# Seven block products for the output projection of the last two batches: fused attention and gated MLP on one core

## The chip, the core and the metric

The kernel runs on one core of a Trainium2 chip: TensorE (PE) multiplies matrices into PSUM, VectorE (DVE), ScalarE (ACT) and GpSimd (POOL) work element by element, and the queue of SyncE (SP) issues nearly all DMAs. The metric is device time in microseconds (us) of one execution, as the median of several runs; lower is better.

## The reference

```python
scores = scale * np.matmul(q, k.transpose(0, 1, 3, 2))      # 4 batches, 12 heads, 448 tokens, 64 wide
scores = np.where(mask, -1000000000.0, scores)              # causal
attn = np.exp(scores - np.max(scores, axis=-1, keepdims=True))
attn = attn / (np.sum(attn, axis=-1, keepdims=True) + 1e-09)
x = np.matmul(attn, v)      # -> (B * S, H * D): 1792 tokens x 768
g = x @ w_gate              # 768 x 1536
silu = g * (1.0 / (1.0 + np.exp(-g)))
return silu * (x @ w_val) @ w_out     # w_out: 1536 x 768
```

All inputs and the output are float32.

## The kernel before, in words

**Tiling.** A batch is one chunk of T = 448 tokens. Activations lie transposed, features on 128 partitions and tokens along the row, so a matmul is 128x128 weights by 128x448 activations. Every float32 operand is split into a high part (a rounded copy) and a low part (operand minus high part), and each product takes three matmuls: high by high, high by low, low by high (`mm3`, L1150 to L1152). The copy runs on ACT, DVE or POOL (`copies`, L400, L403, L406), the subtraction on DVE or POOL (`binary`, L422, L425). A weight tile is 128x768 (`wraw` the raw tile, `whl` its two parts, four buffers each), kept in DRAM as `wr`.

**Stages.** Attention of batch b runs beside the MLP of batch b-1. For batches 0 and 1, `moe` does gate, up and output projection. The last two batches, A = 2 and B_ = 3, share their gate and up products: `early` (L1274) computes the block for A alone, spills partial sums to DRAM (`ks`), and `pair` (L1390) does the rest in five further block products for each of n = 0 to 5, over sums of weights (S1 to S4, `S1hl` and so on their split parts) and sums of activations that `operands` (L1323) prepares (`T2hl`, slabs of the tile `last`). The results are the hidden activations: hA (batch 2; twelve tiles f) and hB (batch 3; in `xs` and `hraw` buffers).

**Output projection of batches 2 and 3.** It is a matrix product in 2x2 by 2x2 blocks: upper and lower half of the 768 output rows (3 tiles m each), first and second half of the 1536 hidden features (6 tiles f each), batch A and B_. Eight block products of 3 x 6 x 3 = 54 matmuls do it. Two of them, first half of the features of A for all six m, run in `early` as soon as these features exist (PSUM tiles MO2_0 to MO2_5, then ACT copies them to `part` and SP spills them as `ko`). The other six run in `outputs` (L1574): for every m, A's second half (with `back`, the spilled part, added by DVE at L1606) and both halves of B_.

**What sets the order.** Every engine works through its instructions in program order. That order is written by `Planner.run`, a list scheduler that plays the kernel through with a cost table: at each step it takes, on the engine that can start earliest, the first ready operation by due time. A due time is written by hand (the stage lengths LEN, the leads WLEAD and BOOST) plus an offset for each group (the table SHIFT, some 300 numbers). Operations that may run on several engines go to the one that would end earliest. Buffers come in rings (CAPS: `whl` 4, `wraw` 4, `wide` 3, `tmp` 2, `t` 2, `osb` 2); an operation that needs a buffer waits for the last user of the oldest.

**Turned heads.** For batches in VIA the softmax weights are transposed through DRAM (`turn`, L862): DVE writes the tile `w`, SP sends it out, SP reads it back. For an odd head the returned data goes into a second buffer, `x`.

## Time and profile before

| what | value |
|---|---|
| runs | 634.48, 634.03, 632.47 us, median 634.03 |
| profiled execution | 632.45 us, of which the span from first to last instruction is 630.7 us |
| granted TensorE clock | 1.00 in all stages (the upper of its two levels, 2.4 GHz) |
| PE busy | 623.1 us, 99% of the span |
| DVE, ACT, POOL busy | 517.0 (82%), 416.9 (66%), 251.3 (40%) |
| DMA | 136.07 MB, mean 216 GB/s |

In the profile PE is the matmuls and PEld the weight loads of TensorE. Matmul durations overlap, since matmuls are pipelined; the distance from one start to the next tells their pace. An engine's waits are listed by what ended them.

### The profile page before, as it was taken

What the parts mean: (1) busy time and instruction counts of PE and PEld (TensorE: products, weight loads), DVE (VectorE), ACT (ScalarE), POOL (GpSimd) and SP (SyncE); (2) the same over time, 40 slices, a digit from 0 to 9 for tenths busy, and PEclk for the clock granted to TensorE, in tenths of its full rate; (3) what the DMA queues carried; (4) which work ended last, traced back from release to release, by engine and by line L of the source; (5) the groups of instructions that cost most, each with busy time, mean ns of one, the idle gap of its engine ahead of it and who ended that gap; (6) DMA issues with size and microseconds to landing.
All of it is one profiled execution on the core that took longest, in us unless ns stands there. A gap on an engine that the chain in (4) does not pass through costs nothing.

```text
span 630.7 us, 11116 instructions
## 1 busy us (share of the span) xinstructions
PE 623.1 (99%) x3590; PEld 561.2 (89%) x3590; DVE 517.0 (82%) x1168; ACT 416.9 (66%) x1001; POOL 251.3 (40%) x301
## 2 busy tenths in 40 slices
PE   8999999999999999999999999999999999999997
PEld 5557999999999999999999998889999999999997
DVE  5998999989998998988998889799988889975210
ACT  6998658958997678577687899775554454561110
POOL 3665543444356455435445453440034324440000
PEclk9999999999999999999999999999999999999999
DMA  8979597888996987576677877886444343236301
GB/s 284 333 245 335 139 384 276 281 318 293 307 362 167 320 267 246 149 249 220 177 224 252 271 239 201 251 283 230 136 121 130 129 131 102 86 109 190 105 18 70
DMA packets 72666, 136.07 MB, mean 216 GB/s; under 512 B 18080, under 2 KB 45472, under 8 KB 72608
## 3 DMA queue, kind: packets, MB, share of 16 engines
q1 hardware_dynamic: 72304, 135.04, 65.5%
q8 instruction: 28, 0.46, 0.3%
q10 hardware_dynamic: 304, 0.33, 0.2%
q14 instruction: 30, 0.25, 0.1%
HBM read 98.34 MB, written 37.00 MB: 215 GB/s over the span
## 4 chain that ended last, share of the span: by engine, by line
PE 83%; DVE 6%; DMA 5%; ACT 4%; issue 1%; POOL 0%; ACTq 0%; SPq 0%; DVEq 0%; POOLq 0%
PE M L1150 10%; PE M L1151 10%; PE M L1152 10%; PE MO L1150 9%; PE MO L1151 9%; PE MO L1152 9%; PE S L618 7%; PE O L1017 5%; DMA wr<-wr 3%; PE T L842 2%; PE O L1062 2%; PE Bb L1467 2%; PE Bb L1466 2%; PE Bb L1468 2%; PE Be L1468 1%
## 5 line engine op out<-in xcount | busy, mean ns | idle before, releaser
L1150 PE MATMUL M<-xh,whl 128*128 128x448 f32 x360 | 133.7, 371 | 0.9 <-ACT s L1289 0.7
L1152 PE MATMUL M<-xh,whl 128*128 128x448 f32 x360 | 130.4, 362 | 0.0
L1151 PE MATMUL M<-xl,whl 128*128 128x448 f32 x360 | 130.4, 362 | 0.0
L422 DVE TENSOR_TENSOR whl<-wraw,whl 128x768 fp32r<-128x768 f32 x86 | 83.9, 983 | 21.1 <-ACT whl L400 20.7
L681 ACT ACTIVATE p<-p,m 128x192 f32<-128x192 f32 (+3 forms) x180 | 91.1, 509 | 2.3 <-DVE m L669 2.0
L400 ACT ACTIVATE whl<-wraw 128x768 fp32r<-128x768 f32 x72 | 60.2, 840 | 34.1 <-PE MO L1152 19.8
L1150 PEld LDWEIGHTS M<-xh,whl 128*128 128x128 f32 x360 | 67.5, 188 | 7.8 <-ACT s L1289 2.8
L1152 PEld LDWEIGHTS M<-xh,whl 128*128 128x128 f32 x360 | 67.5, 187 | 4.7
L669 DVE CUSTOM_DVE_ANT_0 p<-S,masks 128x192 f32<-128x192 f32 (+3 forms) x180 | 68.3, 424 | 3.5 <-PE S L618 3.3
L1151 PEld LDWEIGHTS M<-xl,whl 128*128 128x128 f32 x360 | 67.6, 188 | 3.8
L1150 PE MATMUL MO<-h,whl 128*128 128x448 f32 x162 | 59.7, 369 | 0.0
L1151 PE MATMUL MO<-h,whl 128*128 128x448 f32 x162 | 58.7, 362 | 0.0
L1152 PE MATMUL MO<-h,whl 128*128 128x448 f32 x162 | 58.5, 361 | 0.0
L735 ACT ACTIVATE p<-p,rec 128x192 f32<-128x192 f32 (+3 forms) x128 | 53.9, 478 | 4.6 <-DVE rec L692 4.5
L1136 DVE SCALAR_TENSOR_TENSOR wraw<-wide,top 128x768 uint32<-128x768 uint32 x36 | 36.0, 1000 | 1.9 <-ACT top L400 1.8
L900 DVE STREAM_TRANSPOSE w<-p 128x256 f32<-128x256 f32 (+2 forms) x120 | 36.3, 354 | 0.6 <-ACT p L735 0.3
L618 PEld LDWEIGHTS S<-KS,QS 64*128 64x128 f32 (+1 forms) x432 | 29.6, 174 | 6.3 <-issue 4.1
L681 ACT ACTIVATION_READ_ACCUMULATOR p<-p,m 128x1 f32 (+1 forms) x180 | 34.1, 190 | 0.0
L425 POOL TENSOR_TENSOR whl<-wraw,whl 128x768 fp32r<-128x768 f32 x16 | 29.5, 1848 | 9.2 <-DVE whl L422 3.1
L1150 PE MATMUL MO<-last,whl 128*128 128x448 f32 x90 | 33.1, 368 | 0.0
L1151 PE MATMUL MO<-last,whl 128*128 128x448 f32 x90 | 32.6, 363 | 0.0
L1152 PE MATMUL MO<-last,whl 128*128 128x448 f32 x90 | 32.6, 362 | 0.0
(386 smaller groups left out, 1527.5 us busy)
## 6 DMA issues: line engine op xcount, KB each, us to landing
wide<-in_w_dram SPq DMA_DIRECT2D x36, 768.0 KB, 6.8
wraw<-wr SPq DMA_DIRECT2D x66, 384.0 KB, 4.1
wr<-wraw SPq DMA_DIRECT2D x36, 384.0 KB, 4.2
wr<-wr SPq DMA_DIRECT2D x24, 384.0 KB, 3.8
x<-dO SPq DMA_DIRECT2D x12, 608.0 KB, 6.0
vraw<-in_v_dram SPq DMA_DIRECT2D x24, 256.0 KB, 4.4
qraw<-in_q_dram SPq DMA_DIRECT2D x23, 224.0 KB, 5.0
kraw<-in_k_dram SPq DMA_DIRECT2D x23, 224.0 KB, 5.0
```

Of the source, the lines that this page charges most:

```text
L400: nc.scalar.activation(out(), in_(), AF.Copy, scale=scale)
L422: r["DVE"] = (cost("DVE", "two", n), lambda: nc.vector.tensor_tensor(out(), a(), b(), alu))
L618: nc.tensor.matmul(st[u + y][f"S{i}"][:r], Q[:, q0 : q0 + r], K[:, :q1_] if y else K[:, S - q1_ :], start=z == 0, stop=z == len(passes) - 1)
L669: nc.vector.tensor_tensor_reduce(p[:r], s[f"S{i}"][:r], mask[:r, maskX - q0 : maskX - q0 + q1_] if h % 2 else back[:r, P - min(q1_, P) : P ...
L681: nc.scalar.activation(p[:r], p[:r], AF.Exp, bias=peak(i)[:r], scale=-1.0, accum_out=sums[u % NR][:r, i : i + 1],)
L735: nc.scalar.activation(p[:r], p[:r], AF.Copy, scale=rec[u % NR][:r, i : i + 1])
L900: nc.vector.transpose(to, src)
L1017: nc.tensor.matmul(o, s["VS"][:, j, :m], p, start=x == 0, stop=x == len(todo) - 1)
L1136: nc.vector.scalar_tensor_tensor(w["raw"].bitcast(U32), z, 13, top, ALU.logical_shift_right, ALU.bitwise_or)
L1150: nc.tensor.matmul(out[:, :n], a[:, w], xhi, start=first, stop=False, skip_group_check=True)
L1151: nc.tensor.matmul(out[:, :n], a[:, w], xlo, start=False, stop=False, skip_group_check=True)
L1152: nc.tensor.matmul(out[:, :n], l[:, w], xhi, start=False, stop=bool(last), skip_group_check=True)
```

## The change

The output projection of the two batches takes seven block products. `early` keeps one (upper rows, first half, batch A: MO2_0 to MO2_2 in place of MO2_0 to MO2_5), and `outputs` does six, phase0 to phase5, each over sums or differences of weight blocks (`So`, `top`, added in place from phase to phase) and of activation blocks (`xs`, `T1hl`, `hraw` tiles). The sums are VectorE or GpSimd instructions like the splits (`binary`; `minus` is a new form of the subtraction, on VectorE alone). Three PSUM results run through several phases: ScalarE copies a state out (`ou2`, `ou3`) before the next product adds to it. To have batch 2's hidden features for the sums, `early` and `pair` spill them (`kh`), and SP reads six of the twelve back into `xs`. Some signs change (`activate` takes a sign). The constant ACC is empty, so the DMA branch `gather` isn't used.

An odd head's turned weights return to the buffer that they left from. The planner runs three times: after a pass, `latest` works out for each operation the latest start that delays nothing in that pass, and this is the due time of the next; SHIFT, with new numbers throughout, is added in the last pass alone. `place_all` fixes the order of the buffers in memory. The diff, cut:

```diff
-LEN = [57.293, 137.864, 266.214, 76.452, 83.944, 91.479]
+LEN = [57.293, 137.864, 266.214, 76.452, 83.944, 75.0]
...
+PASSES = 2
 SPARE = [2]
-PLACES = {(1, 1): 7}
+PLACES = {(1, 1): 0}
...
-    "": 0.77, "attention0": -24.87, "attention1": -21.61, "attention10": 3.28, "attention11": 4.59, "attention12": 0.29, "attention13": -0.26,
...
+    "": 0.17, "attention0": -6.39, "attention1": -3.11, "attention10": -1.47, "attention11": -7.66, "attention12": -0.15, "attention13": 0.08,
...
+    def latest(self, order):
+
+        end, after = max(o.end for o in order), None
+        for o in sorted(order, key=lambda o: o.start)[::-1]:
+            t = end
+            for d in o.outs:
+                lag = 0.0 if o in d.soft else o.extra + (LAT[o.eng] if d.eng != o.eng else (0.0 if o.eng == "PE" else 0.13))
+                t = min(t, d.late - lag)
+            for r in o.uses:
+                if r.next is not None:
+                    t = min(t, r.next.owner.late - o.extra - LAT[o.eng])
+            if o.eng == "PE":
+                if after is not None:
+                    t = min(t, after.late)
+                after = o
+            o.late = t - (o.end - o.start)
+
     def run(self, caps):
+        nd, extra = [o.nd for o in self.ops], [o.extra for o in self.ops]
+        order = self.once(caps)
+        for i in range(PASSES):
+            self.latest(order)
+            for o, n, x in zip(self.ops, nd, extra):
+                o.nd, o.extra, o.due = n, x, o.late + (o.shift if i == PASSES - 1 else 0.0)
+                for r in o.uses:
+                    r.left, r.end, r.next = len(r.users), 0.0, None
+            order = self.once(caps)
+        return order
...
-        spare = lambda a, n: [Res(f"lent{a}")] if at is not None else [Res("wide")]
-        rS = spare(4, 3) if odd else spare(0, 4)
+        rS = [Res(f"lent{2 * at + odd}")] if at is not None else [Res("wide")]
...
-        rd = op({"SP": (0.35, back), "kb": ND // 2}, due(6.6), [wr], rP if odd else [], [rD] + ([] if odd else rS))
+            s["turned"] = s["w"][:, :ND]
+            nc.sync.dma_start(s["turned"], s["d"])
+        rd = op({"SP": (0.35, back), "kb": ND // 2}, due(6.6), [wr], [], [rD] + rS)
...
+    def minus(n, out, a, b):
+
+        return {"DVE": (cost("DVE", "two", n), lambda: nc.vector.scalar_tensor_tensor(out(), a(), -1.0, b(), ALU.mult, ALU.subtract)), "port": True}
...
-    keepO = [dpool.tile([P, T], F32, tag=f"ko{m}", name=f"ko{m}") for m in range(KD)]
+    keepO = [dpool.tile([P, T], F32, tag=f"ko{m}", name=f"ko{m}") for m in range(HK)]
+    keepH = [dpool.tile([P, T], F32, tag=f"kh{f}", name=f"kh{f}") for f in range(NF)]
...
-        for m in range(KD):
+            kept["h", f] = spill(keepH[f], lambda f=f: ps[A, f, "t"], at(4 * f + 6), t3, rt)
+        for m in range(HK):
...
+                kept["h", f] = spill(keepH[f], lambda: ps["t21", n], at(9), t3, rt)
...
+        def first_sum(k):
+            res = [Res(f"xs{2 * k}"), Res(f"xs{2 * k + 1}")]
+            ld = op({"SP": (0.3, lambda: nc.sync.dma_start(xs[k], keepH[k])), "kb": 224}, at(HK) - AHEAD - 6, [kept["h", k]], res)
...
+                 op(binary(T, lambda: xs[k], lambda: xs[k], t_, ALU.add), at(HK) - AHEAD + 0.1 * k, [ld, o], [], res + r_))
...
+            a = op(copies("sbuf", T, to[0], lambda: xs[k], -1.0), at(HK) - AHEAD + 1 + 0.1 * k, [d], alloc[:1], res + (rs[:1] if not alloc else []))
+            l = op(minus(T, to[1], lambda: xs[k], lambda: raw(to[0]())), at(HK) - AHEAD + 2 + 0.1 * k, [a], alloc[1:],
+                   res + rs[:1] + (rs[1:] if not alloc else []))
...
+        def second_sum(k):
...
+                 op(binary(T, lambda: xs[k], lambda: xs[k], t_, ALU.add), at(2 * HK) - AHEAD + 0.1 * k, split + [o], [], res + r_))
+            to = (lambda: xh[k], lambda: xl[k])
+            ops_[2, k], places[2, k] = halves(lambda: xs[k], to, at(2 * HK) - AHEAD + 1 + 0.1 * k, [d], res, [Res(f"xh{k}"), Res(f"xl{k}")]), to
...
+        def third_sum(k):
...
+                 op(binary(T, t_, t_, t2, ALU.add), at(3 * HK) - AHEAD + 0.1 * k, [o, o2, sums_["x", k][0]], [], r_ + r2))
+            to = (lambda: hh("T3", k), lambda: hl("T3", k))
+            ops_[3, k], places[3, k] = halves(t_, to, at(3 * HK) - AHEAD + 1 + 0.1 * k, [d], r_, [Res(f"hh{k}"), Res(f"hl{k}")]), to
...
+        def plain(k):
...
+            ops_[4, k], places[4, k] = halves(t_, to, at(4 * HK) - AHEAD + 0.1 * k, [o], r_, rs), to
...
+        def fourth_sum(k):
...
+                d = op(binary(T, lambda: xs[k], lambda: raw(hh("A2", k)), lambda: xs[k], ALU.add), at(5 * HK) - AHEAD - 2 + 0.1 * k, split + [a], [], res + [ra])
+                d = op(binary(T, lambda: xs[k], lambda: xs[k], lambda: raw(hl("A2", k)), ALU.add), at(5 * HK) - AHEAD - 1 + 0.1 * k, [d, l], [], res + [rl])
...
+            ops_[5, k], places[5, k] = halves(lambda: xs[k], to, at(5 * HK) - AHEAD + 0.1 * k, [d], res, [Res(f"xh{k}"), Res(f"xl{k}")], -1.0), to
...
+        def divide(key, src, due, deps, res):
...
+            a = op(copies("sbuf", WC, new, src), due - 6 * WLEAD, deps, [rhl], res)
+            l = op(binary(WC, lambda: hls[key][:, 1], src, lambda: raw(hls[key][:, 0])), due - 5 * WLEAD, [a], [], res + [rhl])
+            return [a, l], rhl
...
+        def phase0(m):
+            src, ld, rw = fetch((0, m), W(m, 1), at(m) - 12 * WLEAD)
+            wo, rhl = divide((0, m), src, at(m), [ld], [rw])
+            rc = Res("MMS"[m])
+            last = product(0, m, ("c", m), "MMS"[m], rc, True, lambda k: (hA[k + HF], (lambda: hh("A2", k), lambda: hl("A2", k))), wo, rhl, [])
...
+            result(A, m, at(m + 1), [last, ld], [rc, rp], lambda: ps["c", m][:, :T], lambda: ps["back", m], scale=-0.5)
...
+        def phase1(m):
+            if "S" not in ACC:
+                s2, l2, r2 = fetch((1, m), W(m + HK, 0), at(HK + m) - 13 * WLEAD)
+                s3, l3, r3 = fetch((2, m), W(m + HK, 1), at(HK + m) - 13 * WLEAD)
...
+                d = op(binary(WC, new, s2, s3, ALU.add), at(HK + m) - 8 * WLEAD, [l2, l3], [rS], [r2, r3])
+            wo, rhl = divide((1, m), lambda: sums_[m], at(HK + m), [d], [rS])
+            re_ = Res("STO"[m])
+            last = product(1, m, ("e", m), "STO"[m], re_, True, lambda k: (ops_[1, k], places[1, k]), wo, rhl, [])
...
+        def phase2(m):
+            src, ld, rw = fetch((3, m), W(m, 0), at(2 * HK + m) - 12 * WLEAD)
+            wo, rS = sums_["s", m]
+            d = op(binary(WC, lambda: sums_[m], lambda: sums_[m], src), at(2 * HK + m) - 8 * WLEAD, [ld, *wo], [], [rS, rw])
...
+            last = product(2, m, ("b", m), "XXM"[m], rb, True, lambda k: (ops_[2, k], places[2, k]), wo, rhl, [])
+            ld, rp = back[m]
+            B = lambda: ps["b", m][:, :T]
+            g = op({"DVE": (two, lambda: nc.vector.scalar_tensor_tensor(B(), ps["back", m], 2.0, B(), ALU.mult, ALU.add))}, at(2 * HK + m + 1) - BOOST,
+                   [last, ld], [], [rb, rp])
+            ru = Res("vraw")
+            u = scaled(("ou2", m), "vraw", "vraw", ru, B, at(2 * HK + m + 1), [g], [rb])
+            upper[m] = (u, rb, ru)
...
+        def phase3(m):
+            s2, l2, r2 = fetch((4, m), W(m, 0), at(3 * HK + m) - 13 * WLEAD)
+            s3, l3, r3 = fetch((5, m), W(m + HK, 0), at(3 * HK + m) - 13 * WLEAD)
+            d = op(binary(WC, s3, s2, s3), at(3 * HK + m) - 8 * WLEAD, [l2, l3], [], [r2, r3])
...
+            last = product(3, m, ("b", m), None, rb, False, lambda k: (ops_[3, k], places[3, k]), wo, rhl, [u2])
+            ru3 = Res("tmp" if m else "t")
+            u3 = scaled(("ou3", m), "tmp" if m else "t", "tmp", ru3, B, at(3 * HK + m + 1), [last], [rb])
+            pe, re_ = lower[m]
+            e = result(B_, m + HK, at(3 * HK + m + 2), [pe, u3], [re_, ru3], lambda: ps["e", m][:, :T], lambda: ps["ou3", m])
...
+        def phase4(m):
+            src, ld, rw = fetch((6, m), W(m, 1), at(4 * HK + m) - 12 * WLEAD)
+            wo, rS = sums_["s", m]
+            d = op(binary(WC, lambda: sums_[m], src, lambda: sums_[m]), at(4 * HK + m) - 8 * WLEAD, [ld, *wo], [], [rS, rw])
...
+            last = product(4, m, ("e", m), None, re_, False, lambda k: (ops_[4, k], places[4, k]), wo, rhl, [e])
+            _, _, ru, u2 = upper[m]
+            result(B_, m, at(4 * HK + m + 1), [last, u2], [re_, ru], lambda: ps["e", m][:, :T], lambda: ps["ou2", m])
...
+        def phase5(m):
+            src, ld, rw = fetch((7, m), W(m + HK, 1), at(5 * HK + m) - 12 * WLEAD)
+            wo, rhl = divide((5, m), src, at(5 * HK + m), [ld], [rw])
+            u3, rb, _, _ = upper[m]
+            last = product(5, m, ("b", m), None, rb, False, lambda k: (ops_[5, k], places[5, k]), wo, rhl, [u3])
+            result(A, m + HK, at(5 * HK + m + 1), [last], [rb], lambda: ps["b", m][:, :T], final=m == HK - 1)
...
```

On PE, the end of the first half's projection in `early` is where the removed products stood. MO2_m is the PSUM tile of output tile m of batch 2, h its features, Be0_0 the first product of pair 0. Before:

```order
L1151 MATMUL MO2_3_6087<-h9_5929,whl102_5977 128x448
L1152 MATMUL MO2_3_6087<-h8_5911,whl102_5977 128x448
L1150 MATMUL MO2_3_6087<-h10_5983,whl102_5977 128x448
L1151 MATMUL MO2_3_6087<-h11_6001,whl102_5977 128x448
L1152 MATMUL MO2_3_6087<-h10_5983,whl102_5977 128x448
L1466 MATMUL Be0_0_6172<-last2_5282,S1hl0_6147 128x448
L1467 MATMUL Be0_0_6172<-last2_5282,S1hl0_6147 128x448
L1468 MATMUL Be0_0_6172<-last2_5282,S1hl0_6147 128x448
```

Now, at the same place:

```order
L1198 MATMUL MO2_2_6098<-h2_5620,whl100_6014 128x448
L1196 MATMUL MO2_1_6078<-h8_5953,whl98_5932 128x448
L1197 MATMUL MO2_1_6078<-h9_5971,whl98_5932 128x448
L1198 MATMUL MO2_1_6078<-h8_5953,whl98_5932 128x448
L1518 MATMUL Be0_0_6115<-last2_5386,S1hl0_6096 128x448
L1519 MATMUL Be0_0_6115<-last2_5386,S1hl0_6096 128x448
L1520 MATMUL Be0_0_6115<-last2_5386,S1hl0_6096 128x448
```

Pair 0 begins beside MO2_1 and MO2_2, where it began between MO2_3 and MO2_5; MO2_3 to MO2_5 are gone from this place.

On DVE, a stretch in the last stage. Before, it splits weight tiles (`whl`, the low part) and adds up outputs (`osb`):

```order
L1606 SCALAR_TENSOR_TENSOR osb2_1_7349<-MO2_1_7273,back1_7248 128x448
L422 TENSOR_TENSOR whl136_7344<-wraw136_7241,whl136_7344 128x768
L422 TENSOR_TENSOR whl139_7373<-wraw139_7292,whl139_7373 128x768
L403 TENSOR_SCALAR whl138_7414<-wraw138_7313 128x768
L1606 SCALAR_TENSOR_TENSOR osb2_2_7420<-MO2_2_7375,back2_7266 128x448
L422 TENSOR_TENSOR whl138_7414<-wraw138_7313,whl138_7414 128x768
```

Now, around the split of phase 2's first weight tile (hl2_0):

```order
L481 TENSOR_TENSOR hraw5_7177<-hraw5_7177,xs5_76 128x448
L481 TENSOR_TENSOR xs4_75<-xs4_75,hraw4_6958 128x448
L481 TENSOR_TENSOR hl2_0_7362<-So0_7156,hl2_0_7362 128x768
L1240 SCALAR_TENSOR_TENSOR T1hl1_7144<-xs4_75,T1hl0_7139 128x448
L481 TENSOR_TENSOR xs3_74<-xs3_74,h7_6834 128x448
L481 TENSOR_TENSOR xs4_75<-xs4_75,hraw4_6958 128x448
L481 TENSOR_TENSOR xs5_76<-xs5_76,hraw5_7177 128x448
L481 TENSOR_TENSOR h7_7388<-hraw3_6789,h6_7366 128x448
```

Between the splits of weights now stand sums of activations and the low parts of these sums, which the products of the same phases wait for.

## Rows read from the trace of the kernel before

**Rows 1.** The page's first part: busy us (share of the span) and instructions.

```profile
PE 623.1 (99%) x3590; PEld 561.2 (89%) x3590; DVE 517.0 (82%) x1168; ACT 416.9 (66%) x1001; POOL 251.3 (40%) x301
```

**Rows 2.** Windows: busy us and instructions by engine, clock, DMA share, GB/s.

```profile
core 0: us, PE busy (x) PEld busy (x) DVE busy (x) ACT busy (x) POOL busy (x), PEclk, DMA share, GB/s
0.00:45.00 45.00, 42.55 (x304) 25.75 (x306) 36.49 (x130) 38.95 (x126) 24.75 (x44) 1.00 0.88 301
45.00:376.00 331.00, 330.62 (x2019) 304.10 (x2016) 299.15 (x738) 256.82 (x652) 158.11 (x188) 1.00 0.79 258
376.00:480.00 104.00, 103.03 (x541) 94.33 (x540) 92.33 (x180) 68.23 (x140) 33.54 (x37) 1.00 0.66 203
480.00:507.00 27.00, 27.00 (x136) 25.03 (x134) 21.59 (x31) 12.45 (x21) 10.09 (x9) 1.00 0.33 113
507.00:536.00 29.00, 28.90 (x145) 27.03 (x145) 25.13 (x36) 13.15 (x22) 10.64 (x10) 1.00 0.39 126
536.00:560.00 24.00, 24.00 (x122) 22.50 (x121) 19.54 (x29) 13.49 (x23) 9.57 (x10) 1.00 0.32 102
560.00:585.00 25.00, 25.00 (x127) 23.43 (x126) 14.49 (x19) 8.66 (x14) 4.65 (x4) 1.00 0.51 159
585.00:630.70 45.70, 42.05 (x211) 39.06 (x209) 8.31 (x11) 5.14 (x8) 0.00 (x0) 1.00 0.17 59
```

**Rows 3.** Timeline of PE in pair 5: start us, us, instruction.

```profile
563.28 0.36 PE L1466 MATMUL Be<-xh,S4hl 128*128 128x448 f32 x1
563.48 0.36 PE L1467 MATMUL Be<-xl,S4hl 128*128 128x448 f32 x1
563.68 0.36 PE L1468 MATMUL Be<-xh,S4hl 128*128 128x448 f32 x1
```

**Rows 4.** Waits of the weight loads: total us, times, longest.

```profile
PEld M L1150 <- ACT s L1289: 2.8, 5, 0.8
```

**Rows 5.** Timeline of DVE in pair 5 and after it.

```profile
541.22 0.95 DVE L422 TENSOR_TENSOR S1hl<-S,S1hl 128x768 fp32r<-128x768 f32 x1
542.09 0.95 DVE L422 TENSOR_TENSOR S2hl<-top,S2hl 128x768 fp32r<-128x768 f32 x1
...
568.04 0.61 DVE L422 TENSOR_TENSOR hraw<-hraw,xs 128x448 f32<-128x448 f32 x1
568.58 0.95 DVE L422 TENSOR_TENSOR whl<-wraw,whl 128x768 fp32r<-128x768 f32 x1
...
570.02 2.54 DVE L422 TENSOR_TENSOR whl<-wraw,whl 128x768 fp32r<-128x768 f32 x2
```

**Rows 6.** Timeline of POOL at the last of these.

```profile
569.69 1.16 POOL L425 TENSOR_TENSOR xl<-hraw,xh 128x448 fp32r<-128x448 f32 x1 [2.59 <-DVE whl L422]
```

**Rows 7.** The page's sixth part: DMA issues, KB each, us to landing.

```profile
wraw<-wr SPq DMA_DIRECT2D x66, 384.0 KB, 4.1
```

**Rows 8.** Timeline of the program's end.

```profile
626.68 0.36 PE L1152 MATMUL MO<-xh,whl 128*128 128x448 f32 x1
627.13 0.54 ACT L400 ACTIVATE osb<-MO 128x448 f32<-128x448 f32 x1 [10.62 <-PE MO L1152]
627.71 0.35 ACTq L1230 DMA_DIRECT2D out_dram<-osb  x1
```

263 lines of the change are left out of this document (186 added, 77 removed), and 101 rows, old and new, of the table SHIFT.

## The prediction

> **What bounds the kernel now.** I read the page's shares first, then a table of windows, then the pace of the matmuls, then who waits. TensorE is busy for 99% of the span [rows 1]. Busy alone says little of an engine whose instructions overlap, so look at the pace: in pair 5 one matmul of 448 columns starts every 0.20 us, each lasting 0.36 us [rows 3], and the stretch 560 to 585 holds 127 of them in 25.0 us, 0.197 us each [rows 2]. The Trainium skill ("Perfetto Trace Analysis", section "Identifying the Most-Contended Engine") says that matmul busy time is no good measure and the share of weight loads is. By that rule the 89% of PEld would leave a tenth of TensorE's time free, and a removed matmul would bring 0.9 of its pace, 1.1 us less in all than below. The trace disagrees for this kernel: the stretch that runs without a gap has 23.43 of 25.00 us of weight loads, so 94% is already the ceiling here, and the lower mean comes from attention's short matmuls. From 376 us on TensorE has few waits; the one of weight is 2.8 us for ScalarE's copies in `early` [rows 4]. The clock is at its upper level throughout [rows 2], and I expect no change there. So TensorE's work sets the time, and VectorE comes second: 92.33 of 104.0 us from 376 to 480, 25.13 of 29.0 later, and only after 585 us nearly nothing [rows 2].
>
> **What the change removes.** One block product, 3 x 6 x 3 = 54 matmuls, in `early`; the order has 3420 rows on TensorE for 3474. At 0.20 us [rows 3] that is 54 x 0.20 = 10.8 us, all on the path that sets the end, since TensorE has no idle time to absorb it. `early` also loses three weight tiles (load, split) and three copies and spills, off the path.
>
> **What it adds, VectorE first.** Uncontended, one of its instructions takes 0.54 us on 128x448 (568.04 to 568.58) and 0.87 us on 128x768 (541.22 to 542.09), start to next start [rows 5]. I count in the order from pair 5's first PSUM update (when its S2 product is done) to the low part of the last weight tile: 105 VectorE instructions, where the old kernel had 44 from the same point to its last split. They are 71 of 448, 31 of 768 and 3 of 384 (0.47): 38.3 + 27.0 + 1.4 = 66.7 us. TensorE has 387 matmuls between the same points, 77.4 us. On average 10.7 us are free; but the order needs results on the way. From the first product of phase 0 to the first of phase 2, TensorE has 123 matmuls, 24.6 us; VectorE, from the split before the one (hl0_0) to the split before the other (hl2_0), has 23 of 448 and 14 of 768: 12.4 + 12.2 = 24.6 us. Nothing is left there. GpSimd makes it worse: beside one GpSimd instruction of 1.16 us [rows 6] two weight splits took 2.54 us for 0.87 + 0.95 [rows 5], 0.72 us more. Five of GpSimd's last eleven instructions fall in this stretch, 3.6 us. Some of it falls into VectorE's own waits, and TensorE can take another ready product; I take **3.0 us** of new TensorE waiting in the last stage. Bounds: 0, if the average slack of 10.7 us covers it all; and 14.1 us, if VectorE gets no faster than in 480 to 507, 27.0 us for 31 instructions, 0.87 each with its waits [rows 2]: 105 x 0.871 = 91.5, less 77.4.
>
> The Trainium skill ("SBUF — State Buffer", section "Who interferes with whom") states that a VectorE instruction with two SBUF inputs and a reading GpSimd instruction exclude each other for the whole instruction, the second one blocking. The 0.72 us agrees in kind: less than the full 1.16. By the page's full block, eleven instructions would cost an estimated 12.8 us and VectorE would end 2.1 us behind TensorE, in place of my 3.0.
>
> **The stretch before.** Between the first matmul of `early` and pair 1's S2 product the order has 484 TensorE rows for 503 and 190 VectorE instructions for 179: TensorE's time falls by some 19 x 0.20 = 3.8 us (the rest of the 10.8 falls later, where pairs stand less interleaved), VectorE's rises by 11 x 0.513 (92.33 us / 180 instructions) = 5.6 us [rows 2]. VectorE's free time there, 104.0 - 92.3 = 11.7 us, shrinks to 2.3. Part of it was waiting that returns: I take **2.0 us** of new TensorE waits. Bounds: 0, and 9.4 if all 11.7 us were waits that stay.
>
> **The rest, with what covers it.** DMA: twelve spills and six reloads of 224 KB, nine more weight loads of 384 KB, three spills and three reloads fewer: some 6 MB where the DMA share is 0.17 to 0.66 [rows 2]. Hidden; uncovered, one weight load is 4.1 us [rows 7]. On SP's queue the reload of xs4 waits until VectorE has used the old xs4, and phase 3's weight loads (wo5_1, wo4_2) are queued behind; phase 3 needs them some 10 us later, so I cost that at nothing, up to 4.1 us if it fails. ScalarE: some sixty instructions in 77 us, far from full, and new waits of `ou2` and `ou3` on products, each 0.54 us [rows 8], with other PSUM banks to work on: nothing. An odd head's data returning to its own buffer: the read already waits for the write out, so nothing, and a `wide` buffer is free sooner. The end: as before a ScalarE copy and one DMA after the last matmul [rows 8], equal. Planner in passes: it shuffles attention too, which the diff can't price. TensorE idles 2.45 us before 45 us [rows 2] and 2.8 us at the copies [rows 4], so -5.3 us at best; doubling the idle of the first stage gives +2.45. I take 0, since from 45 to 376 us TensorE is busy for 330.62 of 331.0 us [rows 2] and the new order keeps the same matmuls in much the same groups.
>
> **The sum**, against the profiled execution (632.45 us: 630.7 of span, 1.75 around it): 632.45 - 10.8 + 3.0 + 2.0 = 626.65 us. The median of the runs is 1.6 us above this execution, the mean of all four times 0.9; halfway in that I forecast **627.0 us**.
>
> **The rivals.**
> 1. *All of the gain arrives.* TensorE had taken other ready products in the pairs without a gap while VectorE was busy for 25.13 of 29.0 us [rows 2], which speaks for it; the zero slack at phase 2 speaks against. Time: 632.45 - 10.8 = 621.65, down to 618.9 if the wait at the copies goes too. Chance 0.13.
> 2. *The gain is eaten.* VectorE in the last stage goes at the pace of 536 to 560, 24.0 us / 29 = 0.828 each [rows 2]: 86.9 us, 9.5 behind TensorE. 632.45 - 10.8 + 2.0 + 9.5 = 633.2: no change. For it: hardly an instruction there is free of a wait. Against: that pace was set by TensorE, VectorE being busy for 19.54 of the 24.0. Chance 0.13.
> 3. *Slower.* VectorE becomes the bound of the last stage: every sum waits for its split, its weight load and GpSimd, and its pace is the 0.871 of 480 to 507. 14.1 us behind: 632.45 - 10.8 + 2.0 + 14.1 = 637.75. It decides from (77.4 + 8.8) / 105 = 0.82 us for each VectorE instruction; beyond 0.84 the kernel is measurably slower. Chance 0.11.
> 4. *It doesn't do what it says*: the 54 matmuls go, but VectorE already sets the pace before pair 1, so the time there stays (9.4 us back, and 3.0 later): 634.05, no change. VectorE's 92.33 of 104.0 us is for it, TensorE's 103.03 against. Chance 0.03.
>
> **How the numbers follow.** My forecast, some of the gain given back (622 to 631.5), has 0.60. The range of 621.0 to 634.0 leaves out most of rival 1's lower part, rival 3 and little else, about 0.2. A measurement of this kernel tells about 0.3%, 1.9 us, from no change. Faster by more: 0.60 + 0.13 = 0.73; within: 0.13 + 0.03 = 0.16; slower: 0.11.
>
> **What would show it.** In the changed kernel's profile: 54 matmuls fewer, still 0.20 us apart; waits of PEld in the last stage for VectorE's low parts (hl2_0, T1hl, xl) of some 3 us in total; VectorE busy to within a few us of the end, where it was nearly idle after 585 us; pair 1 starting 2 to 4 us sooner. Wrong would be: waits of TensorE above 9 us in the last stage, a weight load (wo) as the releaser, or a change in the stages before 376 us larger than 3 us.

## The result, and the profile after

The changed kernel took 625.49 us, the median of 4 runs (624.57 to 625.79), beside 633.25 us for the kernel before (632.17 to 634.48): a ratio of 0.9874, 95% interval 0.985 to 0.9899. That is faster by more than the 0.3% that can be told from no change, and 1.5 us under the forecast of 627.0. The profiled execution took 625.25 us (span 623.1), where the one before took 632.45 (630.7).

The page's first part, as in [rows 1]:

```profile
PE 611.8 (98%) x3536; PEld 551.6 (89%) x3536; DVE 545.3 (88%) x1214; ACT 437.9 (70%) x1035; POOL 249.3 (40%) x311
```

54 matmuls fewer, and 28 us more of VectorE. The windows that answer to [rows 2]:

```profile
376.00:480.00 104.00, 101.85 (x539) 93.69 (x538) 95.98 (x184) 72.71 (x155) 35.47 (x39) 1.00 0.63 206
480.00:507.00 27.00, 27.00 (x137) 25.30 (x136) 23.64 (x38) 11.67 (x21) 4.72 (x5) 1.00 0.46 152
507.00:536.00 29.00, 29.00 (x147) 27.18 (x146) 24.96 (x41) 13.96 (x24) 10.18 (x9) 1.00 0.33 111
560.00:585.00 25.00, 23.23 (x114) 20.76 (x113) 23.52 (x36) 11.26 (x19) 4.60 (x4) 1.00 0.52 167
585.00:623.10 38.10, 34.53 (x172) 31.67 (x170) 25.16 (x36) 13.60 (x23) 3.72 (x4) 0.99 0.36 120
```

From 480 to 536 us TensorE is full, as it was. From 560 to 585 us it does 114 matmuls where it did 127, and VectorE beside it went from 14.49 to 23.52 us busy. The waits of the weight loads (as [rows 4]) name who holds it:

```profile
PEld M L1196 <- ACT s L1340: 3.5, 4, 1.2
PEld Nb L1727 <- DVE hl L481: 1.5, 2, 1.1
PEld Nb L1725 <- ACT hl L459: 1.4, 1, 1.4
```

The last, and the longer of the two waits above it, are one place, the first product of phase 2 (Nb0, with the weights hl2_0). TensorE's timeline there, with lines left out:

```profile
569.47 0.37 PE L1727 MATMUL Nc<-h,hl 128*128 128x448 f32 x1
570.83 0.47 PE L1725 MATMUL Nb<-xh,hl 128*128 128x448 f32 x1 [0.99 <-ACT hl L459]
571.14 0.37 PE L1726 MATMUL Nb<-xl,hl 128*128 128x448 f32 x1
572.26 0.47 PE L1727 MATMUL Nb<-xh,hl 128*128 128x448 f32 x1 [0.75 <-DVE hl L481]
```

569.47 to 570.83 is 1.36 us where 0.20 is normal, 571.14 to 572.26 is 1.12: 2.08 us lost at one tile. I sum such **gaps** below: what passes beyond 0.20 us from the start of a 448-column product to the start of TensorE's next instruction. A product at the lower clock, 0.37 us from its successor, so counts with 0.17 us. By this measure the kernel before loses 2.72 us from 376 to 425 us, 0.38 from 425 to 560 and nothing in 560 to 605; the changed one loses 3.47, 0.05 and 2.98. So 10.8 us of matmuls less, 0.75 and 2.98 more of gaps, 0.33 fewer: 7.4 us, against 7.2 measured between the two profiled executions.

ScalarE's and VectorE's timelines at that place (start us, us, instruction) show two separate limits on hl2_0:

```profile
567.47 1.78 ACT L459 ACTIVATE last<-hraw 128x448 fp32r<-128x448 f32 x3 [6.16 <-PE Ne L1727]
569.93 0.84 ACT L459 ACTIVATE hl<-So 128x768 fp32r<-128x768 f32 x1 [0.68 <-PE Nc L1727]
...
568.57 0.96 DVE L481 TENSOR_TENSOR wo<-wo,wo 128x768 f32<-128x768 f32 x1 [1.16 <-DMA wo<-wr]
...
570.71 0.63 DVE L481 TENSOR_TENSOR xs<-xs,hraw 128x448 f32<-128x448 f32 x1
571.25 0.95 DVE L481 TENSOR_TENSOR hl<-So,hl 128x768 fp32r<-128x768 f32 x1
```

Its high part (ScalarE, 569.93) waits until Nc2's last product releases one of the four `whl` buffers; its low part (VectorE, 571.25) stands behind a sum of weights for phase 3, which itself waited 1.16 us for a transfer, and behind three sums of activations.

### The profile page after: what moved, and what is told of

Same layout as the page of the kernel before. It is cut to its first block, busy times and chain, and to the rows that moved or that the text cites. A ratio compares the mean times of both kernels' runs of the same rounds, so it can differ in the third digit from the quotient of the medians.

```text
span 623.1 us, 11119 instructions
## 1 busy us (share of the span) xinstructions
PE 611.8 (98%) x3536; PEld 551.6 (89%) x3536; DVE 545.3 (88%) x1214; ACT 437.9 (70%) x1035; POOL 249.3 (40%) x311
## 4 chain that ended last, share of the span: by engine, by line
PE 81%; ACT 7%; DMA 5%; DVE 3%; issue 2%; POOL 1%; ACTq 0%; SPq 0%; POOLq 0%
PE M L1196 10%; PE M L1198 10%; PE M L1197 10%; PE S L673 6%; PE MO L1196 5%; PE MO L1197 4%; PE MO L1198 4%; PE O L1065 4%; PE Bb L1520 3%; PE Bb L1519 3%; PE Bb L1518 3%; PE Be L1520 2%; PE Be L1519 2%; PE Be L1518 2%; ACT p L736 2%
## 5 line engine op out<-in xcount | busy, mean ns | idle before, releaser
L724 DVE CUSTOM_DVE_ANT_0 p<-S,masks 128x448 f32<-128x448 f32 (+3 forms) x180 | 69.3, 426 | 10.7 <-PE S L673 9.0
L459 ACT ACTIVATE whl<-wraw 128x768 fp32r<-128x768 f32 x68 | 57.0, 839 | 19.5 <-PE M L1198 7.9
L790 ACT ACTIVATE p<-p,rec 128x320 f32<-128x320 f32 (+3 forms) x122 | 55.4, 510 | 2.2 <-DVE rec L747 1.9
L1196 PE MATMUL MO<-h,whl 128*128 128x448 f32 x102 | 38.0, 372 | 0.0
L794 POOL TENSOR_SCALAR p<-p,rec 128x320 f32<-128x320 f32 (+3 forms) x50 | 27.5, 559 | 25.8 <-DVE pl L481 7.1
L1197 PE MATMUL MO<-h,whl 128*128 128x448 f32 x102 | 37.0, 362 | 0.0
L1198 PE MATMUL MO<-h,whl 128*128 128x448 f32 x102 | 36.9, 362 | 0.0
L465 POOL TENSOR_SCALAR top<-wide 128x768 f16<-128x768 bf16 x18 | 19.5, 1083 | 36.2 <-DVE wraw L1182 9.8
L673 PE MATMUL S<-KS,QS 64*128 64x448 f32 (+3 forms) x432 | 32.3, 295 | 0.0
L1065 PE MATMUL O<-ph,VS 128*128 128x448 f32 (+3 forms) x144 | 30.8, 303 | 0.0
```

The source lines that it names most:

```text
L459: nc.scalar.activation(out(), in_(), AF.Copy, scale=scale)
L673: nc.tensor.matmul(st[u + y][f"S{i}"][:r], Q[:, q0 : q0 + r], K[:, :q1_] if y else K[:, S - q1_ :], start=z == 0, stop=z == len(passes) - 1)
L724: nc.vector.tensor_tensor_reduce(p[:r], s[f"S{i}"][:r], mask[:r, maskX - q0 : maskX - q0 + q1_] if h % 2 else back[:r, P - min(q1_, P) : P ...
L790: nc.scalar.activation(p[:r], p[:r], AF.Copy, scale=rec[u % NR][:r, i : i + 1])
L1065: nc.tensor.matmul(o, s["VS"][:, j, :m], p, start=x == 0, stop=x == len(todo) - 1)
L1196: nc.tensor.matmul(out[:, :n], a[:, w], xhi, start=first, stop=False, skip_group_check=True)
```

## The experiments

"Gaps" are as above. Single executions of nearly the same program differ by a microsecond or more before 390 us (the gap at the first copy `s` stands at 387.42 us in the changed kernel, at 389.10 in x1_release, where the code is the same), so orders of the last stage are compared by their gaps, and times by their ratio to the kernel before, measured on the same chip. Line numbers in the experiments' lines stand up to four higher, and some 55 lower where the table of shifts is empty. The gaps of x9_after_bare are those of the longest of its ten runs (636.90 us).

| kernel | median us | ratio, 95% interval | gaps 376-425 | 425-560 | 560-605 |
|---|---|---|---|---|---|
| changed kernel | 625.49 | 0.9874 (0.985-0.9899) | 3.47 | 0.05 | 2.98 |
| x1_release | 624.29 | 0.9854 (0.9824-0.9884) | 3.44 | 0.0 | 2.91 |
| x2_vector_order | 626.58 | 0.9892 (0.9866-0.9919) | 3.44 | 0.0 | 4.84 |
| x3_both | 628.16 | 0.9911 (0.9877-0.9945) | 3.45 | 0.0 | 6.47 |
| x4_light_sums | 623.58 | 0.984 (0.9817-0.9862) | 3.44 | 0.0 | 2.30 |
| x5_reordered | 628.72 | 0.9934 (0.9915-0.9954) | 3.48 | 0.0 | 7.22 |
| x6_reordered_early | 632.8 | 0.9999 (0.9985-1.0013) | 5.25 | 0.0 | 8.55 |
| x7_fewer_matmuls | 632.31 | 0.9987 (0.9973-1.0001) | 3.57 | 8.25 | 0.0 |
| x8_reordered_again | 624.45 | 0.9866 (0.9842-0.9891) | 3.45 | 0.0 | 3.70 |
| x9_after_bare | 631.79 | 0.9981 (0.9959-1.0003) | 5.25 | 7.22 | 3.93 |
| x10_after_bare_no_passes | 659.4 | 1.0422 (1.0373-1.047) | 16.43 | 9.27 | 3.05 |
| x11_before_bare_passes | 636.92 | 1.0061 (1.0039-1.0082) | 3.18 | 0.51 | 0.0 |
| x12_light_reordered | 621.5 | 0.9831 (0.9796-0.9866) | 3.47 | 0.0 | 0.44 |

### Which of the two limits holds hl2_0

The planner's finished order is taken, and single operations are put ahead of others before the instructions are made (a number is an operation's place of creation; 3222 is Nc2's last product, 3260 Ne1's first, 3291 and 3292 hl2_0's parts, 3283 the first copy into `last`, 3351 the sum of weights for phase 3):

```diff
     order = pl_.run(CAPS)
+    ix = {o.idx: o for o in order}
+    def ahead(at, *what):
+        for a in what:
+            order.remove(ix[a])
+            order.insert(order.index(ix[at]), ix[a])
+    ahead(3260, 3222)
+    ahead(3283, 3291)
```

> The changed kernel, with two instructions' places altered and nothing else: Nc2's last three products stand ahead of Ne1 (so hl0_2's buffer comes free some 5 us sooner), and ScalarE's high part of hl2_0 stands ahead of the three copies into last. Theory 'buffer' (the ring of four weight buffers holds the high part back, and VectorE only follows): the 1.16 us that TensorE lost at the first product of Nb0 goes and the 0.92 us behind it shrinks, 1.0 to 2.0 us in all, a profiled execution of 623.2 to 624.3 us against 625.25. Theory 'VectorE' (the low part comes last by its place in VectorE's queue, started at 571.25 us): the wait for the high part goes, the wait for the low part grows from 0.9 to about 2.0 us in one piece, and the time stays within 0.3 us of 625.25.

The high part's wait went, and the low part's grew to one piece:

```profile
571.07 0.36 PE L1727 MATMUL Nb<-xl,hl 128*128 128x448 f32 x1
572.91 0.47 PE L1728 MATMUL Nb<-xh,hl 128*128 128x448 f32 x1 [1.48 <-DVE hl L482]
```

1.84 us from start to start, and 2.91 us of gaps in all against 2.98. As "VectorE" expected of the waits: the release alone is worth nothing. The profiled execution, 626.35 us, lies above both theories' times.

The other way round, `ahead(3189, 3351, 3377, 3337, 3236, 3338, 3237)`, without the two lines above (3189 is xl5's low part; 3337 to 3237 are the fourth and third sum of tile 3):

> The changed kernel, with four VectorE instructions (the sum of two weight tiles for phase 3, which waited 1.16 us for a transfer, two of the fourth sum of tile 3, one low part of the third sum) moved from ahead of hl2_0's and xl4's low parts to behind them, with the ScalarE copy and the one load that follow from them. Theory 'VectorE': the low part starts as soon as its high part is there, and all that comes behind on VectorE comes 1.2 to 2.5 us sooner; 1.2 us or more is won, at most 624.1 us. Theory 'buffer': the high part still comes at 570.8 us, the low part is done at about 571.8 where it was 572.2, and 0.3 to 0.5 us is won, 624.8 to 625.0 us.

The gaps at Nb0 fell from 2.08 to 1.66 us, the 0.4 that "buffer" expected. Then 1.88 us were lost 13 us further on (2.08 from start to start), at phase 3's first product, which waits for `ou2` (ScalarE's copy of Nb0 after VectorE has added `back` into it; line numbers are one higher here):

```profile
584.27 0.37 PE L1728 MATMUL Nb<-xh,hl 128*128 128x448 f32 x1
586.35 0.47 PE L1726 MATMUL Nb<-h,hl 128*128 128x448 f32 x1 [1.70 <-ACT ou L1752]
```

What was moved back on VectorE now stood ahead of that sum, and on ScalarE a high part that waits for one of VectorE's sums of weights stood ahead of `ou2`. Neither theory had this. A third limit at Nb0 came to light as well: with the sum of weights out of the way, VectorE stood for the reload of `xs`, whose sum is ahead of hl2_0's low part in its order.

```profile
570.01 0.63 DVE L482 TENSOR_TENSOR xs<-xs,hraw 128x448 f32<-128x448 f32 x1 [2.36 <-DMA xs<-kh]
...
584.76 0.84 ACT L460 ACTIVATE hl<-wo 128x768 fp32r<-128x768 f32 x1 [3.83 <-DVE wo L482]
```

Both edits, with 3291 and 3292 ahead of So2's sum (3314), the copies into `last` behind T1hl's high parts and two third sums further back:

> Both edits together, and hl2_0's low part ahead of So2's sum on VectorE, the copies into last behind the high parts of T1hl. Theory 'order' (each of the two holds hl2_0 alone, and neither is a matter of how much work VectorE has): the whole 2.1 us at Nb0 goes and comes back nowhere, 623.0 to 623.4 us, with less than 0.6 us of gaps between 560 and 605 us where there were 3.0. Theory 'pace' (the prediction's own: VectorE has as much work as TensorE from here to the end of phase 3, so what is won at Nb0 is lost again at T1hl, xl or the next weights): only the 1.16 us that VectorE itself stood waiting for the transfer is won, 624.0 to 624.2 us, and new gaps of 1 us or more stand between 571 and 600 us, with VectorE as releaser.

At Nb0 nothing is left of the 2.08 us, so these limits together explain that place. But "order" falls: a wait of 3.2 us came back at `ou2`, and the total is worse than either. "Pace" had said that the loss would come back, but not its size (628.27 us on the profiled execution, 624.0 to 624.2 expected). TensorE's windows around the wait (columns as [rows 2]; the column behind POOL is the granted clock):

```profile
584.00:586.00 2.00, 0.00 (x0) 0.00 (x0) 2.00 (x4) 1.28 (x2) 1.37 (x2) 1.00 0.78 217
586.00:588.00 2.00, 1.84 (x6) 1.66 (x7) 1.90 (x3) 2.00 (x6) 0.86 (x1) 0.71 0.80 270
588.00:590.00 2.00, 2.00 (x7) 1.77 (x6) 2.00 (x4) 1.31 (x3) 0.00 (x0) 0.50 0.68 202
590.00:592.00 2.00, 2.00 (x11) 1.85 (x10) 1.42 (x3) 0.67 (x2) 1.16 (x1) 0.93 0.70 207
```

After the wait the clock is at its lower level for a while: the second and third of these windows hold 6 and 7 matmuls, the fourth 11. I come back to that at the end.

### Is it VectorE's amount of work

In the changed kernel's own order, all in-place sums of the last stage over 64 columns (most of these sums are left out of the result):

```diff
+    def few(*fs):
+        return [lambda f=f: f()[:, :64] for f in fs]
...
-            d = op(binary(WC, lambda: sums_[m], lambda: sums_[m], src), at(2 * HK + m) - 8 * WLEAD, [ld, *wo], [], [rS, rw])
+            d = op(binary(WC, *few(lambda: sums_[m], lambda: sums_[m], src)), at(2 * HK + m) - 8 * WLEAD, [ld, *wo], [], [rS, rw])
```

and likewise in phases 3 and 4 and the first to fourth sum.

> The changed kernel in its own order, with all sums of the last stage that are made in place (first to fourth sums, and the sums of weights of phases 2 to 4) over 64 columns only, where they have 448 or 768: 0.4 to 0.8 us less of VectorE for each of some 25 between 555 and 600 us; most of these sums are left out of the result. Theory 'pace': with VectorE far ahead, the 3.0 us of gaps between 560 and 605 us go but for some tenths, 622.3 to 622.8 us. Theory 'buffer': the high part of hl2_0 still waits for the release by Nc2's last product, the first gap of 1.16 us stays, the low part follows at once, and 0.4 to 0.9 us is won, 624.3 to 624.8 us.

2.30 us of gaps, 0.68 less: the first, 1.36 us from start to start, stayed, the second fell from 1.12 to 0.68. That is "buffer" (its time, 623.78 on the profiled execution, lies half a us under that theory's range). The sums that the planner put on GpSimd shrink too: from 560 to 605 us VectorE is busy for 31.18 us in place of 42.30, GpSimd for 5.64 in place of 8.32. So the waits of the changed kernel come from two sides, and each side alone hides the other.

Twice more I made the last stage's order by hand, with the same work, now for each engine's own sequence and ordered again by data and buffer dependences. The first:

> The changed kernel with the order of its last stage made by hand so that neither limit stands at Nb0 and VectorE never stands waiting: Nc2's last products ahead of Ne1; on ScalarE hl2_0's, T1hl's and xh4's high parts ahead of the copies into last; on VectorE the sums of weights for phases 2 and 3, of the fourth sum and of the third sum behind hl2_0's, T1hl's and xl4's low parts, the sums into Nb ahead of a sum of weights for phase 3, and on SyncE the two loads for the first sum ahead of three weight loads. The work is the same. Theory 'pace' (VectorE has no time to spare from 560 to 597 us, so of the 3.0 us of gaps it can give back only the 1.16 us that it waited for a transfer, and whatever slack stands behind): 1.2 to 1.6 us less than 625.25, 623.6 to 624.1 us on the profiled execution, with the rest of the gaps at Nb's phase 3 or at its weights. Theory 'order' (each wait was a matter of place): nearly all 3.0 us, 622.2 to 622.8 us. Third: a wait of 2 to 3 us for ou2 at Nb0, as where both limits were lifted by the coarser moves, and no gain.

It failed at what I had put on ScalarE: hl2_1's high part stood behind copies that wait for VectorE (1.84 us from start to start), and `ou2` behind hl3_1's high part (2.59 us, the third possibility, and the lower clock behind it). With two of `early`'s copies `s` (2072 ahead of 2451, 2128 ahead of 2581) moved as well:

> The same, and two of ScalarE's copies s (out of TensorE's two M banks, 408 and 387 us) moved ahead of normalisations of p and of two splits that stood in front of them. Theory 'each gap counts by itself': the gaps of 0.55 and 1.03 us go, a further 1.0 to 1.6 us less than the kernel without the two moves. Theory 'given back' (VectorE and the attention's turn set the pace up to pair 1, as the prediction had it for the matmuls removed here): the attention's instructions that were put back cost as much, and the two kernels agree within 0.4 us.

The 1.23 us gap at the copy became 1.0, and the next one, whose copy now stood behind what had been put back, became 2.27:

```profile
408.48 0.47 PE L1196 MATMUL M<-xh,whl 128*128 128x448 f32 x1 [0.63 <-ACT s L1340]
411.26 0.48 PE L1196 MATMUL M<-xh,whl 128*128 128x448 f32 x1 [1.92 <-ACT s L1340]
```

Of the gain expected nothing came, and 1.8 us more of gaps did: given back, and more. The last stage lost another 1.3 us of gaps, since the lower clock came twice there. The second order, with ScalarE's mistakes mended:

> The changed kernel with its last stage's order made by hand a second time. As in the first such order hl2_0 waits for neither limit; what cost there is put right: on ScalarE hl2_1's high part stands ahead of the copies that wait for VectorE's sums, and ou2 ahead of hl3_1's high part (that order put it behind a sum that came late, a 2.6 us wait after which TensorE ran some matmuls 0.37 us apart); on VectorE hl2_1's low part directly behind its high part, the sums into Nb as soon as Nb's product ends. The work is the same. Theory 'order': hardly a gap over 0.5 us between 560 and 605 us, 2.0 to 2.6 us less than the changed kernel, a profiled execution of 622.6 to 623.3 us. Theory 'pace': VectorE is full from 569 us on, and 1.2 us at most is won (its own wait for a transfer), at least 624.0 us, with one new wait of about 1 us behind hl2_1, the sums into Nb or hl3_1. If again a gap over 2.5 us stands anywhere, matmuls 0.37 us apart follow it and the time is over 625 us.

Up to 584 us there is no gap worth the name. Then these, each behind an instruction of VectorE or a copy that waits for one:

```profile
585.50 0.47 PE L1727 MATMUL Nb<-h,hl 128*128 128x448 f32 x1 [0.58 <-DVE hl L481]
587.44 0.48 PE L1726 MATMUL Nb<-h,hl 128*128 128x448 f32 x1 [0.66 <-DVE h L481]
590.43 0.47 PE L1725 MATMUL Nb<-h,hl 128*128 128x448 f32 x1 [1.10 <-ACT ou L1751]
```

3.70 us in all, and a ratio that can't be told from the changed kernel's. "Order" had said under 0.5 us for any of them. The test of what is left, the light sums in this order:

> The second order made by hand, with the sums of the last stage that are made in place over 64 columns only (most of these sums are left out of the result, as in the run with light sums in the changed kernel's own order). The second order alone took the gaps at Nb0 away and had 3.7 us of gaps behind them, at hl3_1, at a tile of the third sum and at ou2; the light sums alone left the 1.16 us at the release of a buffer. Theory 'pace' (VectorE's amount of work up to the end of phase 3 sets where TensorE can be, and the orders only choose at which instruction it shows): with less of it in an order without the buffer's wait the gaps between 560 and 605 us go nearly all, under 0.8 us, and the profiled execution takes 619.5 to 620.5 us. Theory 'order' (the gaps behind Nb0 are misplaced instructions and releases like the first): they stay within 1 us of 3.7, 622 us or more.

0.44 us of gaps remain, of 3.70. All that waits for VectorE from 560 to 605 us is (total us, times, longest):

```profile
PEld Ne L1728 <- DVE osb L1743: 0.5, 1, 0.5
PEld Nb L1730 <- DVE hl L481: 0.2, 1, 0.2
```

The engines' busy time from 560 to 605 us, in the changed kernel and in this run (VectorE is the third column):

```profile
560.00:605.00 45.00, 43.14 (x212) 39.08 (x211) 42.30 (x61) 21.65 (x36) 8.32 (x7) 1.00 0.51 164
...
560.00:605.00 45.00, 44.91 (x225) 41.61 (x224) 31.21 (x64) 19.57 (x34) 5.23 (x6) 1.00 0.46 156
```

The profiled execution took 621.08 us, 0.6 over the range of "pace", with no gap to show for the 0.6. So four kernels: own order 2.98, own order with light sums 2.30, order by hand 3.70, order by hand with light sums 0.44. Taking away VectorE's work is worth 0.7 us in an order that waits for a buffer, and 3.3 us in one that does not. So two things stand behind the 3 us, and either alone keeps most of them: at Nb0 the limits of the planner's order (2.30 us stay with a quarter of VectorE's work gone), and behind them VectorE's amount of work, which puts the gaps elsewhere once that place is mended (3.70). With both out of the way they go.

### What the matmuls are worth by themselves

The kernel before, and of each of the three early products that the change removes only the first group of three matmuls is issued, 45 fewer in all (three partial sums are incomplete; their weight tiles are still loaded and split):

```diff
-                mm3(ps[key], i, f % KD, T, hi, lo, x == 0, x == len(fs) - 1)
+                few = key[1:2] == ("part",) and m >= HK
+                if few and x:
+                    return
+                mm3(ps[key], i, f % KD, T, hi, lo, x == 0, few or x == len(fs) - 1)
```

> The kernel before, and nothing of the change but its matmuls: of the 54 that the change takes from the early output products of batch 2, 45 are left out (of the three products that go, only the first group of three matmuls is issued, so three partial sums are incomplete). Theory 'TensorE alone' (the first term of the prediction's sum): 45 x 0.20 = 9.0 us less, 623.2 to 623.7 us on the profiled execution against 632.45. Theory 'partly given back' (the prediction's second term: 2.0 of 10.8 us lost again before pair 1, since VectorE, ScalarE and the copies there are no faster): 7.0 to 8.0 us less. Theory 'VectorE sets the pace there' (the fourth rival): less than 3 us.

Nearly nothing: a ratio of 0.9987, and 1.3 us between profiled executions of the 9.0. That is what the fourth rival expected (less than 3 us). 8.25 us of gaps appeared between 425 and 507 us: 4.5 at pair 0's first weights, S1hl, 2.4 in the products right behind, which ran at the lower clock, and 1.1 at the S1hl of two later pairs:

```profile
443.77 0.37 PE L1152 MATMUL MO<-h,whl 128*128 128x448 f32 x1
446.93 0.47 PE L1469 MATMUL Be<-last,S1hl 128*128 128x448 f32 x1 [2.79 <-ACT S1hl L400]
...
448.86 0.74 PE L1471 MATMUL Be<-last,S1hl 128*128 128x448 f32 x1 [1.18 <-DVE S1hl L422]
```

```profile
446.00:454.00 8.00, 5.89 (x16) 4.64 (x17) 8.00 (x14) 5.79 (x10) 0.00 (x0) 0.59 0.37 115
```

VectorE's timeline tells why: S1hl's low part in this run, in the kernel before and in the changed one:

```profile
447.86 0.95 DVE L422 TENSOR_TENSOR S1hl<-S,S1hl 128x768 fp32r<-128x768 f32 x1
```

```profile
448.02 0.95 DVE L422 TENSOR_TENSOR S1hl<-S,S1hl 128x768 fp32r<-128x768 f32 x1
```

```profile
438.77 0.95 DVE L481 TENSOR_TENSOR S1hl<-S,S1hl 128x768 fp32r<-128x768 f32 x1
```

In the kernel before, taking the matmuls away moved VectorE by 0.16 us: it was at its own pace, with TensorE just fitting in. In the changed kernel the same low part comes 9.25 us sooner. So the gain needs both: TensorE with less to do, and VectorE at pair 0 sooner. The first alone brought 0.8 us here; the second alone could win little, since TensorE lost only 3.1 us from 376 to 560 us before. What brings VectorE there sooner, the traces tell. Here are the windows from 376 us to the low part, before and after, and the group of GpSimd's low parts of weight tiles in the first of them:

```profile
376.00:448.02 72.02, 71.05 (x381) 64.36 (x380) 63.90 (x137) 51.49 (x111) 24.95 (x29) 1.00 0.75 231
376.00:438.77 62.77, 60.62 (x333) 55.04 (x332) 57.73 (x123) 50.20 (x116) 25.57 (x30) 1.00 0.78 250
```

```profile
L425 POOL TENSOR_TENSOR whl<-wraw,whl 128x768 fp32r<-128x768 f32 x4 | 7.4, 1851 | 1.6 <-DVE pl L422 1.3 <-ACT whl L400 0.3
```

VectorE has 14 instructions and 6.2 us less to do up to that point, and 3.1 us less idle time. It makes twelve low parts of weight tiles in both kernels, and three high parts less (1.7 us); GpSimd's low parts are gone from this stretch. In their place GpSimd makes six of nine sums for the operands of the pairs (into `top` and `T`) that VectorE made alone before, an estimated 6 x 0.54 = 3.2 us of VectorE's time. So the removed tiles made room on GpSimd more than on VectorE, and the new order used it; whether it would have done so with the tiles still there, no run shows. Nor does a run have this order with the old block products.

### The planner

Both kernels with the table of shifts empty, so that no order is tuned: the changed kernel (`SHIFT = {}`), the same without the two passes (`PASSES = 0`), and the kernel before with the changed one's `latest`, `run` and `once`.

> The changed kernel with its table of shifts emptied (two passes of the planner stay). Theory 'block products' (54 matmuls fewer are what counts, and any reasonable order passes the gain on): 626 to 630 us. Theory 'order' (the gain arrives only in an order fitted to it): within 3 us of the kernel before or slower, 630 us or more. Either way the gaps between TensorE's instructions are longer than the changed kernel's, and they show what the table is worth.

> The same with the planner's two passes left out too, so that every instruction keeps its first due time. If the passes carry the gain: 4 us or more longer than with them. If they do not: within 2 us, as the prediction had it, which gave the passes nothing (bounds 5.3 us of gain to 2.5 us of loss).

> The kernel before with its table of shifts emptied and the planner's two passes put in, without the block products. If the passes carry the gain: faster than the kernel before, 628 us or less. If they do not: no faster than before's own tuned order, 632 us or more; the difference to the changed kernel without its table (the run named after_bare) is then what the block products bring between two orders made in the same way, and 'block products' expects 7 to 11 us of it.

Without its table the changed kernel is back at the time of the kernel before, as "order" expected. In that run's trace 7.22 us of gaps stand between 425 and 560 us, nearly all at operands of pair 0 for which TensorE waits (`T2hl`, `last` and `xs` from VectorE, `u` from ScalarE) and in products at the lower clock. Between orders made in the same way the block products bring 636.92 - 631.79 = 5.1 us; "block products" had said 7 to 11. The table is worth 631.79 - 625.49 = 6.3 us to the changed kernel, the passes another 27.6: without them weights and operands come late in several places, as the weight loads' waits show, and the lower clock adds to it (mean granted clock 0.979).

```profile
PEld M L1143 <- DVE whl L426: 10.5, 2, 6.0
PEld Nb L1670 <- ACT h L404: 7.1, 1, 7.1
```

With the passes and no table the kernel before takes 636.92 us, against 633.04 with its own table. So the passes don't bring the gain by themselves, but this code needs them, or due times as good. Two kernels weren't run: the one before with an empty table and no passes, which would tell what the passes are worth to it, and the one before with passes and a table fitted to them, which would tell how much of the gain a new order brings without the block products.

## Why the prediction was right, by its own steps

**54 matmuls at 0.20 us, all on the path: the size right, the reason too simple.** They are gone, and the rest still starts 0.20 us apart. "TensorE has no idle time to absorb it" was the argument, and x7 shows that it isn't enough: in the old order TensorE's idle time appears as soon as its work is taken away. The Trainium skill ("Perfetto Trace Analysis", section "Identifying the Most-Contended Engine") takes the share of weight loads, beside the share of peak arithmetic, for TensorE's load; as before, the trace disagrees: 25.30 of 27.0 us in a window where TensorE is full.

**3.0 us of new waits in the last stage: right to the tenth (2.98), with the place right and the working partly wrong.** Phase 2's first product and hl2_0's low part were named, and x8 and x12 bear out that VectorE's work is one of its two causes. Not seen was the other, the `whl` buffer that held the high part. And GpSimd's five instructions were put at 0.72 us each. They are there (550.0 to 561.0), and the two largest effects are these, with the GpSimd instruction beside the first:

```profile
553.66 1.16 POOL L484 TENSOR_TENSOR xs<-xs,h 128x448 f32<-128x448 f32 x1 [2.50 <-DVE top L481]
554.04 1.27 DVE L1585 SCALAR_TENSOR_TENSOR xs<-tg,xs 128x448 f32<-128x448 f32 x1
562.02 1.38 DVE L481 TENSOR_TENSOR hl<-top,hl 128x768 fp32r<-128x768 f32 x1
```

VectorE's first takes 1.19 us to the next start where 0.54 is normal, the second 1.30 where 0.87 is; with two smaller ones that is 1.4 us for five, not 3.6. The Trainium skill ("SBUF — State Buffer", section "Who interferes with whom") has a VectorE instruction with two SBUF inputs and a GpSimd instruction that reads SBUF contend under an exclusive lock. The trace agrees: VectorE's first starts 0.38 us into the GpSimd instruction (553.66 to 554.82) and ends 0.49 us after it. But what VectorE loses is the rest of that instruction, not all 1.16 us, so eleven of them at the full price were too dear.

From hl0_0's low part (543.16) to hl2_0's (571.25) VectorE took 28.1 us, beside the 24.6 + 3.6 worked out. But it was 1.4 for GpSimd and 1.8 of waits, of which 1.16 were for a transfer that I had costed at nothing. It wasn't the case named there either: this weight load was issued at 564.30, two us ahead of the reload on SP, as soon as an earlier sum of VectorE's had released the buffer, and landed at 568.55. So the agreement to the tenth is luck, the sum of two errors.

**2.0 us before pair 1: 0.75 measured, and the count behind it was wrong.** I took 2.0 between 0 and 9.4 us. The tuned order has 0.75, and 0.33 less behind it; x7 has 8.25 with what is tied to it. I wrote that pair 1 would start 2 to 4 us sooner, since "the rest of the 10.8 falls later": pair 1's first S2 product starts at 464.67 us where it was 473.51, 8.8 us sooner. All of the gain is there by then, and the later stages only give some back. The error lies in the start of the stretch. I counted from `early`'s first matmul, and in the new order that stands among the last products of the batch before, some 5 us sooner (371.78 us, 376.72 before). So unlike stretches were compared. Counted from the start of the program to that S2 product, TensorE has 2777 matmuls for 2825, so 48 of the 54 are gone by then, not 19; and from 376 us to it VectorE is busy for 81.20 us in 161 instructions where it was 85.84 in 172, so its work falls there and doesn't rise by 5.6 us. VectorE was said to be busy to within a few us of the end; its last instruction ends at 612.95, 10 us before it, with 25.16 of the last 38.1 us busy.

**The fourth rival's mechanism was real.** "VectorE already sets the pace before pair 1" had 0.03, with TensorE's 103.03 busy us of 104.0 against it. A TensorE that is full says that it isn't waiting; it doesn't say that what feeds it could be faster. In the order before VectorE was as late as TensorE, and x7 has what that rival forecast, no change (ratio 0.9987). It didn't come true since the change also reorders VectorE.

**Three weight tiles off the path: wrong, as far as the traces tell.** Ahead of S1hl, which sets the pace there, three high parts (1.7 us) are gone from VectorE and the low parts from GpSimd, which takes over sums of VectorE's.

**The planner at 0: not a sum that can be held against one number.** The passes and the table belong to the gain: without the table the changed kernel is no faster than the one before (0.9959 to 1.0003). I priced them as a change beside the others; they are what lets the others arrive. **The rest at 0** (DMA but for that one transfer, ScalarE, the odd heads' buffer, the end) held: the stages up to 376 us lose within 0.3 us of what they lost before. The odd heads' buffer by itself wasn't run.

So the mechanism held in its outline, TensorE's time shorter and a part given back to VectorE's work in the last stage; the error of 1.4 us on the profiled execution (626.65 forecast, 625.25 measured) is nearly all the 2.0 us taken before pair 1, where 0.42 net was lost. That it isn't larger is luck, since the errors within the 3.0 cancelled.

## What to carry to other kernels

When two engines are both nearly full in a stretch (here 99% and 89%), taking work from the first alone is worth what the second lets through: before costing a removed instruction at its full time, find the instruction of the other engine that the next stage waits for, and ask whether it comes sooner. A wait at one place with two releasers was cured by neither cure alone here, and curing both only moved it while the engine behind them was full; cut that engine's work in a run to see how much is amount and how much order. Removing one of several waits by hand in a planned order needs every queue behind the moved instruction looked at, ScalarE's included.
